# Seven tap weights spread by a matmul, and a tile that moves from 256-token steps to a 512-token step

## The chip, the core and the metric

The kernel runs on one core of one Trainium2 chip. The metric is the device time of one execution in microseconds (us): 690.42 for the kernel before, the median of three runs from 689.95 to 690.78. The profiled execution has a span of 688.2 us; all times inside the kernel are counted from the start of that span.

## What is computed

Tokens are rows of 192 numbers; there are 8 sequences of 4096 tokens. A causal convolution with 7 taps, whose weights are a softmax over the taps and differ for each of 8 groups of 24 channels, is followed by a feed-forward block of width 2048 with a Silu whose argument is scaled by a beta for each of its channels.

```python
w = exp(weight - max(weight, -1)); w = w / sum(w)            # weight: 8 groups x 7 taps
conv[b, s, h, :] = sum_k w[h, k] * x_pad[b, s + k, h, :]     # x: 8 x 4096 x 192, 6 zero rows in front
h = conv @ w_in                                              # 192 x 2048
out = (h / (1 + exp(-beta * h))) @ w_out                     # 2048 x 192
```

## The kernel before

Two streams of 16,384 tokens each are worked on side by side; a step of n tokens means n tokens of each stream. The steps are 128, 128 and 256 tokens for the first tile of 512, then 256 tokens up to the end of the fourth tile, then 512 tokens for the other 28 tiles. `pin` keeps an instruction in program order on its engine.

```python
steps = [(0, 128), (128, 128), (256, 256)]
NP = len(steps)
steps += [(t, 256) for t in range(TILE, 4 * TILE, 256)]      # steps 3 to 8
NQ = len(steps)                                              # 9
steps += [(t, TILE) for t in range(4 * TILE, TS, TILE)]      # steps 9 to 36
```

The head of the kernel builds the taps. Each tap weight is wanted on every partition that holds a channel of its group, so a load repeats every row of `weight` eight times for each stream. The Exp of the taps makes seven diagonal matrices; TensorE uses them for the convolution of the first tile, on x that it has transposed itself.

```python
for s, eng in enumerate((nc.sync, nc.scalar)):
    pin(eng.dma_start(out=x0[:, 0, s, :], in_=xs[s, 0:128, :]))
for s, eng in enumerate((nc.sync, nc.scalar)):
    pin(eng.dma_start(out=taps[half_of(s), :],
                      in_=weight[:, None, :].to_broadcast([H, Q // H, K])))
# ... beta16 and x0[1] follow on sync; w_in, xb0, w_out, xb1, xf on gpsimd
pin(nc.scalar.activation(scrap, one, AF.Exp))                # brings the Exp table in
# ... ident by memset and affine_select
warm(9, 256)                                                 # matmuls on ones
pin(nc.vector.tensor_reduce(out=nmax, in_=taps, axis=AX.X, op=ALU.max, negate=True))
pin(nc.scalar.activation(etap, taps, AF.Exp, bias=nmax, accum_out=tsum))
for k in range(2): make_diag(k)                              # diag[k] = ident2 * etap[:, k]
t = transpose_0(pa[0], x0, 0)                                # 3 TensorE transposes
take_0(t, 0, act=True)                                       # xr <- PSUM, on ScalarE
warm(6, 128)
for k in range(2, K): make_diag(k)
pin(nc.scalar.activation(scrap, one, AF.Silu))               # brings the Silu table in
conv_0(b0, 0)                                                # 7 taps x 2 streams of matmuls
evac_0(b0, 0, 0, nc.scalar); evac_0(b0, 0, 1, nc.vector)     # xcp <- PSUM
t1 = transpose_0(pa[1], x0, 1)
# ... transpose of beta, then first_tile() weaves the other blocks into steps 0 and 1
```

From the second tile on, VectorE does the convolution (`tap`, 7 instructions for a 256-token step, 21 for a 512-token step), up to two steps ahead of TensorE and ScalarE. In a step, `mm1` makes 16 chunks of h, ScalarE applies the Silu to each, and the second product runs one step behind. It has two forms. After a 256-token step it is `mm2`, with tokens as rows of the output, taken out by a VectorE copy. From the step NQ on, the output is transposed (`mm2_quarters`) and taken out by a VectorE stream transpose; this form needs `w_out_q`, a rearranged copy of w_out that VectorE makes once.

```python
for i in range(n_steps):
    plan = mm2_plan(i - 1) if NP <= i <= NQ else [[] for _ in range(NF)]
    for u in range(NF):
        mm1(i, u)                              # 6 or 12 matmuls, then one Silu
        for t in plan[u]: mm2(i - 1, *t)
        if i > NQ: mm2_quarters(NM)
        vector_work(i, 1307 * steps[i][1] // TILE, flush=u == NF - 1)
# the queue of VectorE work: for each step its fetch, at NQ + 1 the w_out_q copies, its conv
    if i == NQ + 1:
        work += [(i, 330, lambda c=c, m=m: part_w_out(c, m)) for c in range(0, NF, 4) for m in range(NM)]
    work += conv_ops(i)
```

Of the kernel before, what the change touches and what calls it, by code (L numbers as in the profile page):

```python
# [10 lines left out]
FP32 = mybir.dt.float32  # L11
FP32R = mybir.dt.float32r
BF16 = mybir.dt.bfloat16
AF = mybir.ActivationFunctionType
ALU = mybir.AluOpType
AX = mybir.AxisListType
# [3 lines left out]
def kernel(  # L20
# [9 lines left out]
    nc = tc.nc  # L30

    B, S, D = x.shape
    H, K = weight.shape
# [5 lines left out]
    Q = D // NK  # L39
    NS = 2  # L40
    TS = B * S // NS
    TILE = 512
# [3 lines left out]
    def pin(ins):  # L46

        return tc.keep_in_program_order(ins)
# [4 lines left out]
    consts = ctx.enter_context(tc.tile_pool(name="consts", bufs=1))  # L53
# [11 lines left out]

    steps = [(0, 128), (128, 128), (256, 256)]
    NP = len(steps)
    steps += [(t, 256) for t in range(TILE, 4 * TILE, 256)]
    NQ = len(steps)
    steps += [(t, TILE) for t in range(4 * TILE, TS, TILE)]  # L70
    n_steps = len(steps)


# [35 lines left out]
    def half_of(s):  # L109
        return slice(64 * s, 64 * s + 64)  # L110
# [8 lines left out]
    x0 = consts.tile([128, 2, NS, D], FP32, name="x0")  # L119
    xb0 = consts.tile([128, 2, NS, D], BF16, name="xb0")  # L120
    xb1 = consts.tile([128, 2, NS, D], BF16, name="xb1")
    taps = consts.tile([128, K], FP32, name="taps")
    for s, eng in enumerate((nc.sync, nc.scalar)):
        pin(eng.dma_start(out=x0[:, 0, s, :], in_=xs[s, 0:128, :]))  # L124
    for s, eng in enumerate((nc.sync, nc.scalar)):
        pin(eng.dma_start(out=taps[half_of(s), :],
                          in_=weight[:, None, :].to_broadcast([H, Q // H, K])))
    beta16 = consts.tile([NF, 128], FP32, name="beta16")
    pin(nc.sync.dma_start(out=beta16, in_=moe_beta.rearrange("(c p) -> c p", p=128)))
    HF = F // 2  # L130
# [1 line left out]
    def load_x0(b, eng):  # L132
# [7 lines left out]
    scrap = consts.tile([128, 1], FP32, name="scrap")  # L140
    pin(nc.scalar.activation(scrap, one, AF.Exp))

    ident = consts.tile([128, 128], FP32, name="ident")
    pin(nc.vector.memset(ident, 0.0))
    pin(nc.gpsimd.affine_select(out=ident, in_=ident, compare_op=ALU.not_equal, fill=1.0,
                                base=0, pattern=[[-1, 128]], channel_multiplier=1))
    for f0, f1 in ((0, 256), (256, 640), (640, HF)):
# [7 lines left out]
    for s in range(NS):  # L155
        pin(nc.gpsimd.dma_start(out=xb1[:, :, s, :],
                                in_=xs[s, TILE:TILE + 256, :].rearrange("(b p) d -> p b d", p=128)))
# [21 lines left out]
    def warm(n, cols):  # L179
        for _ in range(n):  # L180
            pin(nc.tensor.matmul(idle[:, 0, 0:cols], ones[:, 0:128], ones[:, 0:cols], start=True, stop=True))

    warm(9, 256)
    cv0 = psum_h.tile([128, 2, TILE], FP32, name="ph")
    nmax = consts.tile([128, 1], FP32, name="nmax")
    pin(nc.vector.tensor_reduce(out=nmax, in_=taps, axis=AX.X, op=ALU.max, negate=True))
    etap = consts.tile([128, K], FP32, name="etap")
    tsum = consts.tile([128, 1], FP32, name="tsum")
    pin(nc.scalar.activation(etap, taps, AF.Exp, bias=nmax, accum_out=tsum))  # L189
    diag = consts.tile([128, K, NS, Q], FP32R, name="diag")  # L190

    def make_diag(k):
# [10 lines left out]
    def transpose_0(bank, src, b):  # L203

        bf = src.dtype == BF16
        t = (bank.bitcast(BF16) if bf else bank)[:, 0:NK * 128].rearrange("p (k t) -> p k t", k=NK)
        v = src[:, b, :, :].rearrange("p s d -> p (s d)").rearrange("p (m k) -> p k m", k=NK)
        for kk in range(NK):
            pin(nc.tensor.transpose(t[:, kk, :], v[:, kk, :], ident_b if bf else ident))  # L209
        return t  # L210

    def take_0(t, b, act=False):
        dst = xr[:, :, PAD + 128 * b:PAD + 128 * b + 128]
        if act:
            pin(nc.scalar.activation(dst, t, AF.Copy))  # L215
        else:
            pin(nc.vector.tensor_copy(dst, t))
# [20 lines left out]
    pb = po_banks()  # L238
    t = transpose_0(pa[0], x0, 0)
    take_0(t, 0, act=True)  # L240
    warm(6, 128)
    for k in range(2, K):
        make_diag(k)
    rsum = consts.tile([128, 1], FP32, name="rsum")
# [219 lines left out]
    for i in range(NP, n_steps):  # L464
        j = steps[i][0] // TILE + 1
# [140 lines left out]
```

## Time and profile before

| what | value |
|---|---|
| device time, median of 3 | 690.42 us |
| span of the profiled execution | 688.2 us |
| TensorE matmul (PE) busy | 681.2 us, 99% |
| weight loads (PEld), beside the matmuls | 451.1 us, 66% |
| ScalarE (ACT) busy | 586.5 us, 85% |
| VectorE (DVE) busy | 553.2 us, 80% |
| GpSimd (POOL) busy | 14.1 us, 2% |
| granted TensorE clock, all 40 slices | 0.9 or more |
| first Silu of step 0 / 3 / 9 / 10 / 11 starts at | 11.54 / 34.14 / 97.97 / 114.40 / 135.12 us |

Busy time is an average over stages that differ. The first Silu of a step, read in the timeline of ScalarE, cuts the span into steps; the length of a step is the distance to the next one. In the timeline a line has its start, its length, the engine, the line of the program and the tiles (out<-in), a count where several alike were merged, and in brackets the idle time of the engine before it, with what ended it. SPq, ACTq and POOL lines with DMA are the issue of a transfer, not the transfer.

### The profile page before, as it was taken

How to read it: one execution, taken by the hardware profiler on the slowest of the kernel's cores; microseconds unless marked ns; L12 is line 12 of the kernel's file. 1: busy time of each engine (PE TensorE's matmuls, PEld its weight loads, DVE VectorE, ACT ScalarE, POOL GpSimd, SP SyncE). 2: the span in 40 equal slices, each digit the busy share in tenths (PEclk: the TensorE clock that was granted, in tenths of full speed). 3: DMA queues.
4: the chain of work that ended last, by engine and by line, in shares of the span. 5: the costliest groups of instructions: out<-in, count | busy, mean ns of one | idle time of the engine just before them, and what ended most of it. 6: DMA issues, size and time to landing. Idle time of an engine off the chain costs nothing.

```text
span 688.2 us, 27039 instructions
## 1 busy us (share of the span) xinstructions
PE 681.2 (99%) x12426; PEld 451.1 (66%) x12426; DVE 553.2 (80%) x902; ACT 586.5 (85%) x600; POOL 14.1 (2%) x25
## 2 busy tenths in 40 slices
PE   7999999999999999999999999999999999999998
PEld 5799986555555555555555555555555567777777
DVE  4999999999998889878889888888888898875112
ACT  5999999888888888888888888888888888888881
POOL 7000000000000000000000000000000000000000
PEclk9999999999999999999999999999999999999999
DMA  9554333354334344323344323444224443220113
GB/s 212 157 139 113 89 105 90 89 134 108 102 76 106 105 118 117 80 62 106 105 117 116 79 63 106 105 117 116 72 70 105 106 117 71 56 55 12 48 49 92
DMA packets 148977, 66.84 MB, mean 97 GB/s; under 512 B 110672, under 2 KB 148256, under 8 KB 148864
## 3 DMA queue, kind: packets, MB, share of 16 engines
q1 hardware_dynamic: 145480, 61.08, 34.5%
q0 software_dynamic: 3168, 3.93, 2.7%
q8 instruction: 97, 1.59, 1.0%
q14 instruction: 16, 0.13, 0.1%
q10 hardware_dynamic: 216, 0.10, 0.0%
HBM read 28.32 MB, written 25.17 MB: 78 GB/s over the span
## 4 chain that ended last, share of the span: by engine, by line
PE 97%; ACT 1%; DMA 1%; DVE 0%; issue 0%; SPq 0%; DVEq 0%
PE ph L330 47%; PE po L408 41%; PE po L362 6%; PE po L446 2%; PE ph L313 1%; ACT gp L317 1%; DMA taps<-in_weight_dram 1%; ACT g L317 1%; PE ph L223 0%; PE po L209 0%; PE po L223 0%; ACT etap L189 0%; SPq L124 0%; ACT xr L215 0%; DVE o_sp L368 0%
## 5 line engine op out<-in xcount | busy, mean ns | idle before, releaser
L334 ACT ACTIVATE g<-ph,beta 128x1024 bf16<-128x1024 f32 (+1 forms) x544 | 560.4, 1038 | 79.0 <-PE ph L330 63.4
L330 PE MATMUL ph<-xc,w_in_s 64*64 64x512 bf16 (+2 forms) x5856 | 589.3, 366 | 0.3 <-ACT g L317 0.3
L408 PE MATMUL po<-g,w_out_q 64*64 64x512 bf16 x5184 | 528.5, 376 | 0.0
L330 PEld LDWEIGHTS <-w_in_s 64*64 64x64 bf16 (+1 forms) x5856 | 271.5, 104 | 126.8 <-issue 0.5
L296 DVE SCALAR_TENSOR_TENSOR acc<-xt,tapn,acc 128x512 f32<-128x512 bf16 (+1 forms) x450 | 311.3, 763 | 0.9
L408 PEld LDWEIGHTS <-w_out_q 64*64 64x64 bf16 x5184 | 240.0, 105 | 91.9
L425 DVE STREAM_TRANSPOSE o_sb<-po 128x512 f32<-128x512 f32 x81 | 72.0, 889 | 110.3 <-PE po L408 110.3
L296 DVE SCALAR_TENSOR_TENSOR xc<-xt,tapn,acc 128x512 bf16<-128x512 bf16 (+1 forms) x90 | 64.1, 763 | 0.1
L362 PE MATMUL po<-w_out_s,g 64*128 64x192 bf16 x896 | 57.1, 243 | 0.0
L86 DVE CAST xb<-xf 128x768 bf16<-128x768 f32 (+1 forms) x62 | 48.7, 824 | 0.0
L362 PEld LDWEIGHTS <-g 64*128 64x128 bf16 x896 | 43.4, 94 | 3.3
L294 DVE TENSOR_SCALAR acc<-xt,tapn 128x512 f32<-128x512 bf16 (+1 forms) x90 | 41.0, 488 | 1.1
L368 DVE COPY o_sp<-po 128x192 f32<-128x192 f32 x40 | 12.7, 350 | 9.7 <-PE po L446 7.3
L313 PE MATMUL ph<-xcp,w_in_s 64*128 64x256 bf16 (+1 forms) x144 | 15.0, 316 | 0.2 <-ACT gp L317 0.2
L317 ACT ACTIVATE gp<-ph,beta 128x256 bf16<-128x256 f32 x32 | 12.4, 479 | 1.8 <-PE ph L313 1.8
L446 PEld LDWEIGHTS <-g 128*128 128x128 bf16 x128 | 10.5, 98 | 0.4 <-issue 0.4
L446 PE MATMUL po<-w_out_s,g 128*128 128x192 bf16 x128 | 10.7, 246 | 0.0
L317 ACT ACTIVATE g<-ph,beta 128x512 bf16<-128x512 f32 x16 | 9.6, 692 | 0.2
L313 PEld LDWEIGHTS <-w_in_s 64*128 64x128 bf16 x144 | 6.8, 97 | 3.6 <-issue 1.0
L223 PE MATMUL po<-xr,diag 64*128 64x384 f32 x49 | 8.9, 401 | 0.0
L362 PE MATMUL po<-w_out_s,gp 64*128 64x192 bf16 x128 | 7.2, 243 | 0.0
L362 PEld LDWEIGHTS <-gp 64*128 64x128 bf16 x128 | 5.8, 94 | 1.6
(49 smaller groups left out, 60.1 us busy)
## 6 DMA issues: line engine op xcount, KB each, us to landing
xf<-in_x_dram SPq DMA_DIRECT2D x60, 384.0 KB, 3.9
out_dram<-o_sb SPq DMA_DIRECT2D x108, 192.0 KB, 4.6
out_dram<-o_sp SPq DMA_DIRECT2D x16, 192.0 KB, 4.1
xt<-xb SPq DMA_TRANSPOSE x122, 3.0
w_out_f<-in_moe_w_out_dram POOLq DMA_DIRECT2D x4, 384.0 KB, 7.3
w_in_s<-w_in_s POOLq DMA_DIRECT2D x4, 192.0 KB, 6.0
out_dram<-o_sp SPq DMA_DIRECT2D x8, 96.0 KB, 1.6
w_in_s<-in_moe_w_in_dram POOLq DMA_DIRECT2D x4, 144.0 KB, 4.9
```

The source lines that it names most:

```text
L86: pin((eng or nc.vector).tensor_copy(xbf_of[j][:, b0:b1, :, s, :].rearrange("p b k q -> p k b q"), xf_of[j][:, b0:b1, s, :].rearrange("p b ...
L294: pin(nc.vector.tensor_scalar_mul(a, src, w))
L296: pin(nc.vector.scalar_tensor_tensor(out=xc_of[i][:, k0:k1, 0:n] if k == K - 1 else a, in0=src, scalar=w, in1=a, op0=ALU.mult, op1=ALU.add))
L313: pin(nc.tensor.matmul(ph[:, h, 0:NS * n], w_in_s[half_of(h), kk, ts(fcs[h], 128)], xc_of[i][half_of(h), :, kk, :], start=(kk == 0), stop= ...
L317: pin(nc.scalar.activation(g_at(i, fcs[h])[:, :, 0:n], ph[:, h, 0:NS * n].rearrange("p (s t) -> p s t", s=NS), AF.Silu, scale=beta[:, fcs[ ...
L330: pin(nc.tensor.matmul(ph[m0:m1, s, 0:n], w_in_s[half_of(s), kk, 128 * fc + m0:128 * fc + m1], xc_of[i][half_of(s), kk, 0:n], start=(kk == ...
L334: pin(nc.scalar.activation(g_at(i, fc)[:, :, 0:n], ph[:, :, 0:n], AF.Silu, scale=beta[:, fc:fc + 1]))
L362: pin(nc.tensor.matmul(po[q][:, 0:D], g_at(i, fc)[r, s, ts(b, 128)], w_out_s[r, fc, :], start=(phase == 0 and fc == 0), stop=(phase == 1 a ...
L368: pin(nc.vector.tensor_copy(dst, po[:, 0:D]))
L408: pin(nc.tensor.matmul(po_of[i, m][half_of(s), 0:n], w_out_q[half_of(r), fc, m, :], g_at(i, fc)[half_of(r), s, 0:n], start=(first and fc = ...
L425: pin(nc.vector.transpose(osb_of[i][:, 0:n // L, :, m], po_of[i, m][:, 0:n].rearrange("p (b l) -> p b l", l=L)))
L446: pin(nc.tensor.matmul(po[:, 0:D], g_at(i, fc)[:, s, ts(b, 128)], w_out_s[:, fc, :], start=(fc == 0), stop=(fc == NF - 1)))
```

## The change

Two independent things are done.

The first is in the head. The taps are loaded as they are, 8 rows of 7 numbers, by one transfer that goes first on its queue. A matrix `sel` of zeros and ones (8 x 128) is built by a memset and a second affine_select, and one matmul `sel` x taps spreads the eight rows over 128 partitions into PSUM, from where the maximum and the Exp read them. Three small warming matmuls follow it, and seven instead of six follow the transposes. The transfer of taps that ScalarE's queue issued is gone, and x0's first half is now the second transfer on sync. It is for starting the convolution of the first block earlier.

The second moves `NQ` from 9 to 7: the fourth tile is one step of 512 tokens in place of two of 256, so that the kernel has 36 steps, 29 of them of 512 tokens. All that hangs on NQ moves along: the first 512-token step (with `mm2` of the step before it) is step 7, `w_out_q` is made in the queue of step 8, and `mm2_quarters` begins in step 8.

```diff
-    steps += [(t, 256) for t in range(TILE, 4 * TILE, 256)]
+    steps += [(t, 256) for t in range(TILE, 3 * TILE, 256)]
     NQ = len(steps)
-    steps += [(t, TILE) for t in range(4 * TILE, TS, TILE)]
+    steps += [(t, TILE) for t in range(3 * TILE, TS, TILE)]
...
-    taps = consts.tile([128, K], FP32, name="taps")
+    taps = consts.tile([H, K], FP32, name="taps")
+    pin(nc.sync.dma_start(out=taps, in_=weight))
     for s, eng in enumerate((nc.sync, nc.scalar)):
         pin(eng.dma_start(out=x0[:, 0, s, :], in_=xs[s, 0:128, :]))
-    for s, eng in enumerate((nc.sync, nc.scalar)):
-        pin(eng.dma_start(out=taps[half_of(s), :],
-                          in_=weight[:, None, :].to_broadcast([H, Q // H, K])))
...
+    sel = consts.tile([H, NS, H, Q // H], FP32, name="sel")
+    pin(nc.vector.memset(sel, 0.0))
     ident = consts.tile([128, 128], FP32, name="ident")
     pin(nc.vector.memset(ident, 0.0))
+    pin(nc.gpsimd.affine_select(out=sel, in_=sel, compare_op=ALU.not_equal, fill=1.0, base=0,
+                                pattern=[[0, NS], [-1, H], [0, Q // H]], channel_multiplier=1))
...
-    pin(nc.vector.tensor_reduce(out=nmax, in_=taps, axis=AX.X, op=ALU.max, negate=True))
+    tap_ps = cv0[:, 1, 0:K]
+    pin(nc.tensor.matmul(tap_ps, sel.rearrange("h s g j -> h (s g j)"), taps, start=True, stop=True))
+    warm(3, 128)
+    pin(nc.vector.tensor_reduce(out=nmax, in_=tap_ps, axis=AX.X, op=ALU.max, negate=True))
-    pin(nc.scalar.activation(etap, taps, AF.Exp, bias=nmax, accum_out=tsum))
+    pin(nc.scalar.activation(etap, tap_ps, AF.Exp, bias=nmax, accum_out=tsum))
...
-    warm(6, 128)
+    warm(7, 128)
```

## The prediction

> **What bounds the kernel now.** I read the chain that ended last first, to see where the span is set; then the timeline of the head; then the steps one by one. The chain in order of time (start, length, what):
>
> ```profile
> 1.19 4.75 DMA taps<-in_weight_dram
> 7.09 0.66 PE ph L223
> 9.70 0.84 PE po L209 x3
> 10.75 1.25 PE ph L313 x12
> 14.92 2.30 ACT gp L317 x6
> ```
>
> The kernel's first 6 us hang on the transfer of seven tap weights. Then come the first convolution (L223), two groups of matmuls, and from 11.54 on the Silus of step 0. From 11.54 to 97.6 ScalarE is busy without gaps worth naming, so there a shift of the first Silu shifts everything. From the first step with quarters on, TensorE sets the pace: 20.72 us a step to the end. So the head counts in full, unless a later load catches it. The timeline of the head:
>
> ```profile
> 0.74 0.39 SPq L124 DMA_DIRECT2D x<-in_x_dram  x1
> ...
> 1.19 0.80 SPq L126 DMA_DIRECT2D taps<-in_weight_dram  x1
> 1.19 1.20 ACTq L126 DMA_DIRECT2D taps<-in_weight_dram  x1
> ...
> 3.44 0.88 PE L209 MATMUL po<-ident,x 128*128 128x128 f32 x3 [0.58 <-DMA x<-in_x_dram]
> ...
> 6.04 0.16 DVE L186 TENSOR_REDUCE nmax<-taps 128x1 f32<-128x7 f32 x1 [4.18 <-DMA taps<-in_weight_dram]
> 6.23 0.30 ACT L189 ACTIVATE etap<-taps,nmax 128x7 f32<-128x7 f32 x1 [2.31 <-DVE nmax L186]
> ...
> 6.53 0.47 ACT L215 ACTIVATE xr<-po 128x384 fp32r<-128x384 f32 x1
> ...
> 7.09 0.66 PE L223 MATMUL ph<-xr,diag 64*128 64x384 f32 x1 [2.14 <-ACT xr L215]
> ```
>
> What to see: the transposes of x were done at 4.32, but their copy to `xr` stands behind `etap` in ScalarE's order, and `etap` behind the taps. TensorE idles 2.14 us on it. The steps, as busy time of each engine in windows cut at the first Silu of steps 7, 8, 9 and 10 (window, length, then busy us and count of PE, PEld, DVE, ACT, POOL):
>
> ```profile
> 76.50:87.10 10.60, 10.60 (x230) 10.57 (x226) 10.10 (x20) 10.52 (x17) 0.00 (x0) 1.00 0.36 88
> 87.10:97.90 10.80, 10.80 (x228) 10.46 (x224) 9.76 (x21) 10.49 (x16) 0.00 (x0) 1.00 0.38 117
> 97.90:114.40 16.50, 16.50 (x235) 10.73 (x232) 16.46 (x34) 16.36 (x16) 0.00 (x0) 1.00 0.34 92
> 114.40:135.10 20.70, 20.70 (x380) 12.43 (x380) 20.63 (x37) 17.82 (x16) 0.00 (x0) 1.00 0.32 81
> ```
>
> The 256-token steps and the first 512-token step are ScalarE's (10.52 of 10.60, 16.36 of 16.50); the quarter steps are TensorE's, ScalarE having 17.82 of 20.70. VectorE is full in both of the last two windows. That matters for the second half of the change.
>
> **What the Trainium skill says.** "DMA: Bandwidth & Descriptors", section "Anatomy of one DMA": a transfer costs about 2.0 us however small, mostly waiting for the write's receipt. The trace has that form: the two halves of x, issued at 0.74, landed at 3.19 and 3.35, that is 2.45 and 2.61 us; the repeated taps, many pieces of 28 bytes, needed 4.75. "ScalarE: Activation LUTs", "What ACT_TABLE_LOAD costs": about 1283 ns; the trace has 1.28 us, twice, in the head. "TensorE: Matmul & The Clock Gate", Part 1: the array runs at half rate until one window of 3.4 us was busy, the windows run freely, and (Part 4) transposes don't count as busy. The trace agrees with a late switch: 256-column matmuls start 213 ns apart up to 11.6 us and 107 ns apart after, and TensorE idled from 2.9 to 3.4 and from 5.0 to 7.1. Nothing in the trace shows that transposes don't count.
>
> **Part 1, the head.** Taps now go out at 0.74. With the 2.45 us of the x half they land near 3.1 (their issue shouldn't exceed that half's 0.39). The x half behind them goes out 0.4 later and lands near 3.6. `sel` needs a memset and a select ahead of `ident`'s (the present select takes 0.29), ready near 1.4, no wait. The spreading matmul I put at 0.25 (the 16-column transpose of beta took 0.28): over at 3.35. `nmax` 0.16 and `etap` 0.30, with the gaps of today (0.06, 0.03): `etap` is over at 3.9. ScalarE is free for it, since its table load no longer stands behind a taps issue of 1.20: today it ran 2.42 to 3.70, now from 1.2 to 2.5. First diagonal at 4.3 (0.13 wait and 0.244 each, 1.71 for seven).
>
> The transposes start at 3.65 and end at 4.5, and now they, not the taps, end the wait of `xr`: 4.55 to 5.05. The seven warming matmuls (0.107 apart) end near 5.3. **The first convolution starts at 5.25 in place of 7.09: 1.85 us earlier.** The added matmul, memset and select lie beside the wait for x.
>
> From there two things decide what arrives. First the clock. If the windows lie as in this trace, they end at 11.6, 8.2 and 4.8. With no long gap after 4.8, the array is at full rate by 8.2 at the latest. The convolution at half rate takes 2.6 us as now (7.09 to 9.70) and ends at 7.85; evacuation 0.65 (Silu table then long loaded); then the first mm1 and Silu, today 0.86 apart, 0.5 at full rate. First Silu at 9.1 in place of 11.54: 2.4 earlier. Were the clock full already by 4.8, the diagonals (0.244 each) would pace the convolution and the first Silu could come near 8.4.
>
> Second, the loads. Landings I worked out from the trace and moved 0.3 later for the second select: first w_in pieces 6.2 and 6.7 (wanted 8.6), x block 1 near 7.0 (wanted 7.85), x blocks 2 and 3 9.2 and 9.7 (wanted from 9.5 and 10.5), last w_in piece 12.4 (wanted by u=5, at 15.07 today, so at 12.6), w_out 13.3 to 17.1 (wanted 13.9 on). A gain of 2.4 just passes; over 2.7 the last w_in piece stops it. **I take 2.2 us**, between the bare 1.85 and 2.4.
>
> **Part 2, the steps.** Two 256-token steps go: first Silus at 65.94 and 87.08, so 21.14 for the pair. One quarter step is added: 20.72 (114.40 to 135.12). **Gain 0.42 us.** The ScalarE-bound first 512-token step of 16.4 is there before and after, only two steps earlier.
>
> Does VectorE keep up? Before, it made `xc` of step 9 by 93.19, 3.7 us ahead, and of step 10 only by the moment it was wanted:
>
> ```profile
> 97.81 1.70 DVE L269 COPY w_out_q<-w_out_s 128x256 bf16<-128x256 bf16 x8
> ...
> 111.28 2.06 DVE L296 SCALAR_TENSOR_TENSOR xc<-xt,tapn,acc 128x512 bf16<-128x512 bf16 x3
> 113.27 1.60 DVE L86 CAST xb<-xf 128x768 bf16<-128x768 f32 x2
> ```
>
> Step 10's mm1 began at 113.52. After the change, in times without the head's shift: VectorE ends conv of step 6 at 57.95 and, with the 16.1 us that casts and conv of step 9 took (76.67 to 93.19 without 0.44 of waiting), has step 7's at 74.0, wanted at 75.6. Then copies of w_out 2.6, casts 1.6, out-copies 1.6 and conv 13.3: step 8's at 93.1. It is wanted at about 92.9 (step 7's first Silu at 76.9 plus 16.0). So VectorE, one tile earlier in its run, is still just in time, or 0.2 late. A stall there is paid in full, as TensorE sets the pace from then on. **I charge 0.2 us.**
>
> **Sum:** 690.42 - 2.2 - 0.42 + 0.2 = 687.99, say 688.0.
>
> **Rivals.**
> 1. The x transfer takes the place of the taps: pushed behind them, it lands later than 3.6, or the seven warming matmuls delay the convolution. For it: the diff puts the taps first on that queue. Each 0.1 us late costs 0.1. If x lands at 4.5, the head gains 1, and the time is 689.2.
> 2. Loads catch the head: w_in and the x blocks arrive 0.3 later, and the gain stops at 1.5 or so. For it: DMA engines are at nine tenths from 3 us on. Against: today nothing after 6 us waits for one on TensorE. The time: 688.7.
> 3. VectorE misses step 8 by more, 1 us or more, because its lead is shorter: every 256-token tile gave it some lead (10.1 of 10.6 busy), and one such tile is gone. The time: 689 to 689.5.
> 4. The clock opens at 4.8: another 0.3 to 0.5, 687.5.
>
> **Range and chances.** The terms I am unsure of are the head (1.5 to 2.8) and the stall (0 to 1). Together they give 687.2 to 689.5; the three runs of before differ by 0.8, so I take 687.0 to 689.6. 2% is 13.8 us, five times the whole effect: within 2% 0.98, faster 0.01, slower 0.01.
>
> **What would show it.** `nmax` no longer waits for a DMA but for TensorE, before 3.7; `xr` is released by the transposes; first convolution at 5.2 to 5.4; 256-column matmuls 107 ns apart from about 8.2; first Silu near 9.2 to 9.5; step 7 of 16.4 and then 20.72 each; little or no wait of TensorE for `xc` at step 8. A DMA wait of TensorE between 9 and 13, or a wait for `xc`, would prove rivals 2 or 3. I'd be wrong altogether if the step period of 20.72 changed, which nothing here touches.

## The result and the profile after

The changed kernel took 686.97 us (median of 4 runs, 686.85 to 687.65) beside 690.6 for the kernel before (4 runs, 689.95 to 690.98): a ratio of 0.995, 95% interval 0.9933 to 0.9968. Repeated with more runs it took 687.25 (22 runs) beside 688.86 (67 runs): 0.9976, interval 0.9966 to 0.9985. So the change is worth about 1.6 us, well within 2%. The time after is the same both times; what moved is the kernel before, whose single runs lie anywhere from 687.0 to 692.7. Part of the reason is shown below; it matters for every number here.

The chain that ended last, in the changed kernel (start, length, what):

```profile
1.75 2.56 POOL w_in_s L113 x4
4.32 4.88 DMA xb<-in_x_dram
12.22 2.30 ACT gp L323 x6
```

The taps are gone from the chain. In their place stands another transfer, the one of x block 2 (`xb`), and ahead of it four issues of w_in on GpSimd's queue. The timeline of the changed head:

```profile
0.74 0.41 SPq L123 DMA_DIRECT2D taps<-in_weight_dram  x1
...
2.79 0.59 PE L190 MATMUL ph<-taps,sel 8*128 8x7 f32 x2
...
3.42 0.17 DVE L192 TENSOR_REDUCE nmax<-ph 128x1 f32<-128x7 f32 x1 [1.20 <-PE ph L190]
...
4.49 0.49 ACT L221 ACTIVATE xr<-po 128x384 fp32r<-128x384 f32 x1 [0.52 <-PE po L215]
...
5.13 0.44 PE L229 MATMUL ph<-xr,diag 64*128 64x384 f32 x1
...
7.47 0.83 PE L319 MATMUL ph<-xcp,w_in_s 64*128 64x256 bf16 x12
...
8.01 1.57 ACT L323 ACTIVATE gp<-ph,beta 128x256 bf16<-128x256 f32 x4 [0.76 <-DVE xr L223]
...
9.24 0.35 PE L215 MATMUL po<-ident_b,xb 128*128 128x128 bf16 x3 [0.94 <-DMA xb<-in_x_dram]
```

What to see: `nmax` waits for TensorE, `xr` for the transposes. The convolution starts at 5.13, and twelve mm1 matmuls take 0.83 in place of 1.32: the array is at full rate. The first Silu comes at 8.01, 3.53 earlier than before. Then, at 9.24, TensorE stands 0.94 us for x block 2. The steps, in windows cut at the first Silus of steps 6, 7, 8 and 9 (length, then PE, PEld, DVE, ACT, POOL busy):

```profile
63.30:74.20 10.90, 10.90 (x231) 10.56 (x226) 10.90 (x23) 10.52 (x17) 0.00 (x0) 1.00 0.42 129
74.20:90.60 16.40, 16.40 (x233) 10.62 (x231) 16.36 (x36) 16.31 (x16) 0.00 (x0) 1.00 0.36 98
90.60:111.40 20.80, 20.80 (x380) 14.79 (x380) 20.73 (x37) 17.88 (x17) 0.00 (x0) 1.00 0.34 82
```

The sequence of steps is the old one, one tile earlier. VectorE has `xc` of step 8 ready just in time; the next cast shows when it was free:

```profile
88.00 2.07 DVE L302 SCALAR_TENSOR_TENSOR xc<-xt,tapn,acc 128x512 bf16<-128x512 bf16 x3
89.99 1.61 DVE L86 CAST xb<-xf 128x768 bf16<-128x768 f32 x2
```

The marks by which all profiles below are compared (us from the span's start):

| kernel | nmax starts | convolution of block 0 | first Silu of step 0 | of step 1 | span |
|---|---|---|---|---|---|
| before, first profile | 6.04 | 7.09 to 9.70 | 11.54 | 17.95 | 688.2 |
| before, second profile | 4.87 | 5.92 to 8.53 | 10.17 | 16.51 | 686.8 |
| changed, first profile | 3.42 | 5.13 to 6.64 | 8.01 | 15.25 | 685.2 |
| changed, second profile | 3.41 | 5.11 to 6.62 | 8.00 | 15.23 | 685.3 |
| before, with warming matmuls | 4.93 | 5.99 to 7.59 | 8.96 | 15.30 | 685.6 |
| changed, without warming | 3.42 | 4.81 to 7.42 | 9.27 | 15.96 | 685.9 |
| third tile at 512 too | 3.41 | 5.13 to 7.59 | 8.96 | 15.30 | 693.5 |
| matrix copied from identity | 3.42 | 5.08 to 6.59 | 7.96 | 14.94 | 684.9 |
| and x block 2 first | 3.41 | 5.11 to 6.63 | 8.00 | 15.09 | 685.1 |

### The profile page after: what moved, and what is told of

Read it like the earlier page. It is cut to its first block, busy times and chain, and to the rows that moved or that the text cites. A ratio compares the mean times of both kernels' runs of the same rounds, so it can differ in the third digit from the quotient of the medians.

```text
span 685.2 us, 26902 instructions
## 1 busy us (share of the span) xinstructions
PE 679.8 (99%) x12368; PEld 501.6 (73%) x12368; DVE 553.0 (81%) x905; ACT 584.0 (85%) x584; POOL 14.6 (2%) x26
## 4 chain that ended last, share of the span: by engine, by line
PE 97%; ACT 1%; DMA 1%; POOL 0%; issue 0%; DVE 0%; POOLq 0%
PE ph L336 47%; PE po L414 42%; PE po L368 4%; PE po L452 2%; PE ph L319 1%; ACT gp L323 1%; DMA xb<-in_x_dram 1%; ACT g L323 1%; POOL w_in_s L113 0%; PE po L229 0%; PE po L215 0%; POOL sel L146 0%; DVE o_sp L374 0%; POOL ident L148 0%; POOLq L146 0%
## 5 line engine op out<-in xcount | busy, mean ns | idle before, releaser
L336 PE MATMUL ph<-xc,w_in_s 64*64 64x512 bf16 (+2 forms) x5856 | 573.2, 369 | 0.3 <-ACT g L323 0.3
L336 PEld LDWEIGHTS <-w_in_s 64*64 64x64 bf16 (+1 forms) x5856 | 303.8, 105 | 95.2 <-issue 0.6
L414 PEld LDWEIGHTS <-w_out_q 64*64 64x64 bf16 x5376 | 289.4, 106 | 72.3
L431 DVE STREAM_TRANSPOSE o_sb<-po 128x512 f32<-128x512 f32 x84 | 74.7, 889 | 113.0 <-PE po L414 112.9
L368 PE MATMUL po<-w_out_s,g 64*128 64x192 bf16 x640 | 40.8, 243 | 0.0
L368 PEld LDWEIGHTS <-g 64*128 64x128 bf16 x640 | 31.0, 94 | 3.3
L374 DVE COPY o_sp<-po 128x192 f32<-128x192 f32 x32 | 10.2, 350 | 7.3 <-PE po L452 7.3
```

What stands on the lines that cost most here:

```text
L336: pin(nc.tensor.matmul(ph[m0:m1, s, 0:n], w_in_s[half_of(s), kk, 128 * fc + m0:128 * fc + m1], xc_of[i][half_of(s), kk, 0:n], start=(kk == ...
L368: pin(nc.tensor.matmul(po[q][:, 0:D], g_at(i, fc)[r, s, ts(b, 128)], w_out_s[r, fc, :], start=(phase == 0 and fc == 0), stop=(phase == 1 a ...
L374: pin(nc.vector.tensor_copy(dst, po[:, 0:D]))
L414: pin(nc.tensor.matmul(po_of[i, m][half_of(s), 0:n], w_out_q[half_of(r), fc, m, :], g_at(i, fc)[half_of(r), s, 0:n], start=(first and fc = ...
L431: pin(nc.vector.transpose(osb_of[i][:, 0:n // L, :, m], po_of[i, m][:, 0:n].rearrange("p (b l) -> p b l", l=L)))
```

## The experiments

**Each half alone.** The edit of the first keeps the old steps in the changed kernel, that of the second makes only the new steps in the kernel before:

```diff
 # head alone (in the changed kernel)      # steps alone (in the kernel before)
-range(TILE, 3 * TILE, 256)               -range(TILE, 4 * TILE, 256)
+range(TILE, 4 * TILE, 256)               +range(TILE, 3 * TILE, 256)
```

> The head of the change alone, with the fourth tile still in two 256-token steps. If the two halves of the change simply add, and the head brought 2.68 us by the first Silu of step 3 (34.14 before, 31.46 after): first Silus of steps 0 to 3 as in the changed kernel (8.0, 15.25, 21.9, 31.5), span 688.2 - 2.7 = 685.5, and 2.7 us faster than before. Rival, that the head is paid back later because a stage further on waits for a load or for VectorE: the first Silus of steps 3 to 9 drift back toward those of before, and less than 2 us is left at the end.

> The step half alone, on the old head. First theory (two steps of 10.57 out, one of 20.72 in, and a wait for xc of at most 0.1): 0.35 us faster than before, step 7 of 16.5 us, then 20.72 each. Rival (VectorE's shorter lead costs as much as the step saves, or more): no gain or a loss of up to 0.5, with a wait of TensorE or its weight loads for xc at step 8 of 0.5 or more.

Measured: the head alone 687.47 (21 runs) beside 688.72 (65 runs), ratio 0.9984, interval 0.9977 to 0.9991: 1.1 us, not 2.7. Its profile is as expected, first Silus 7.86, 15.29, 21.95 and 31.48, span 685.6, and nothing drifts back. So the rival isn't the reason: the base was another. The steps alone took 689.29 (13 runs), ratio 1.0008, interval 0.9998 to 1.0018. By the time this is a miss: 0.35 us faster would be 0.9995, outside the interval. The profile shows the gain all the same. From the first Silu of step 3 (33.79) to that of step 8 (92.98) it took 59.19; the kernel before needs for the same tokens 34.14 to 93.68 (114.40 less one step of 20.72), 59.54. That is the expected 0.35. It stands in the other profiles too: from the first Silu of step 1 to the end, the five with the old steps take 670.26 to 670.33, the eight with the new ones (the run with a third tile aside) 669.93 to 670.07. So the step half is worth about 0.3, and whatever else sets these profiles apart lies ahead of step 1. What the head did in the other twelve runs of the steps alone is not known.

**What the first comparison was worth.** The changed kernel, the head alone and the kernel before were run once more, beside each other, unchanged.

> The changed kernel once more, beside runs of the kernel before on the same chip. The first comparison had four runs of each and gave 3.6 us (ratio 0.995); beside the later runs, in which the kernel before took 688.7 and 689.0, the head alone gave 1.2 us. Theory of the varying head (the kernel before differs from run to run by when the taps land, 4.9 to 6.0 in three profiles, and by when the array's rate doubles, while the changed kernel waits for x block 2 near 9.2 whatever happened earlier): changed kernel 686.9 to 687.2 with a spread under 1 us, kernel before near 688.7 with a spread of 4, ratio 0.9972 to 0.9982. Rival (the first four runs were typical): 3 us or more, ratio under 0.9960.

> The head alone once more, to stand beside the changed kernel on the same chip; the two differ in the fourth tile's steps only. Trace theory (21.14 us of two steps give way to 20.72, and the first 512-token step is 0.07 longer): the changed kernel is faster than this by 0.35 us. Rival (the step half is worth nothing, as the run of it alone, 1.0008, could be read): the two are equal within 0.1.

> The kernel before, unchanged, for a second profile of it. Theory of the varying head: ratio 1.000 within 0.001, and the profile's first Silu and taps do not repeat the first profile's 11.54 and 5.98; where the time is 688.5 or below, the taps came earlier or the 256-column matmuls were already 107 ns apart at their first. Rival (the head repeats, and the chips differ): first Silu within 0.2 of 11.54.

Measured: 687.25 (22 runs, all but one within 686.7 to 687.7), ratio 0.9976; head alone 687.64 (14 runs), ratio 0.9986, interval 0.9974 to 0.9997; before against itself 688.94 and 688.86, ratio 1.0006, interval 0.9996 to 1.0016. Changed kernel and head alone lie 0.39 apart in their medians, as the trace's 0.35 says; the intervals alone would not part them. The theory of the varying head holds for the two profiles of the kernel before. In the second:

```profile
4.87 0.16 DVE L186 TENSOR_REDUCE nmax<-taps 128x1 f32<-128x7 f32 x1 [3.01 <-DMA taps<-in_weight_dram]
...
5.92 0.65 PE L223 MATMUL ph<-xr,diag 64*128 64x384 f32 x1 [1.17 <-ACT xr L215]
...
9.51 0.94 PE L313 MATMUL ph<-xcp,w_in_s 64*128 64x256 bf16 x12
```

The taps came 1.17 earlier than in the first profile, and the rate changed in the middle of the twelve mm1 matmuls (0.94, between 1.32 and 0.83). That execution took 688.56, the first 690.01; the first Silu of step 1 came 1.44 earlier, which is the whole difference. In the eight profiles with the new load in which the matrix is not made late, `nmax` starts at 3.41 or 3.42. The change removes a spread as well as a time. Two things stay open: no execution near 687.0 or 692.7 was profiled, and only 10 of these 67 runs are as slow as the fastest of the first four, so why all four were is not known.

**Is it the clock?** The array's rate is read here from the distance between the starts of matmuls. The granted clock of the windows does not show it: in the first profile of before it reads 1.00 from 3 to 8 us, where the pairs of convolution matmuls start 0.32 apart, against 0.18 in the changed kernel. Warming matmuls alone were added to the kernel before, and taken out of the changed one:

```diff
 # in the kernel before                    # in the changed kernel
-warm(9, 256)                             -warm(3, 128)
+warm(9, 256); warm(4, 128)               -warm(7, 128)
-warm(6, 128)
+warm(28, 128)
```

> The kernel before, with the old repeated load of the taps, and only warming matmuls added: four of 128 columns while x is awaited, and 28 in place of 6 while the taps are awaited. The convolution cannot start before 7.1. Clock theory (a good part of the head's gain came because TensorE had no long idle stretch, so its array went to full rate at about 5 in place of 11.6): convolution of block 0 in 1.5 to 1.7 us in place of 2.6, first Silu near 9.7 to 10.1 in place of 11.54, and 1.4 to 1.8 us faster than before. Start theory (the gain is the earlier start alone, the rate changes on its own schedule): first Silu at 11.5 or a little later, time as before within 0.3.

> The changed kernel without the three and the seven warming matmuls. They are left out, nothing else. Clock theory: TensorE then idles from about 4.5 to 5.1 and the array may stay at half rate; the convolution starts at 5.1 all the same but takes 2.6 us, first Silu at 9.2 to 9.6 in place of 8.0; since the loads hold step 0 back to 9.24 anyway, only 0.3 to 0.8 us of time is lost. Rival (half a microsecond of idleness is too short to matter): convolution in 1.3 to 1.5 us, first Silu at 8.0, time as the changed kernel's, 687.0.

The timeline of TensorE in the kernel before with warming:

```profile
3.87 1.81 PE L181 MATMUL ph<-const-bfloat16-1.0 128*128 128x128 bf16 x28
5.99 0.41 PE L224 MATMUL ph<-xr,diag 64*128 64x384 f32 x1 [0.31 <-ACT xr L216]
...
8.42 0.83 PE L314 MATMUL ph<-xcp,w_in_s 64*128 64x256 bf16 x12
9.19 0.35 PE L210 MATMUL po<-ident_b,xb 128*128 128x128 bf16 x3
```

687.8 (21 runs, 687.25 to 688.14), ratio 0.9983, interval 0.9975 to 0.9990: 0.9 us faster and a spread of 0.9 in place of 4.3, by idle work alone. The repeated load of the taps is still there, so its landing alone does not make a spread of 4.3. The convolution took 1.60 in place of 2.61. The taps had come early in this profile (4.93), so the second profile of before is the one to compare with: same taps, 1.21 earlier at the first Silu of step 0 and at that of step 1. The clock theory is right in kind; I expected 1.4 to 1.8. The transposes of x block 2 (the last line) wait for no load here: the block had landed at 8.38. The changed kernel without its warming:

```profile
4.81 0.68 PE L228 MATMUL ph<-xr,diag 64*128 64x384 f32 x1 [0.58 <-ACT xr L220]
...
8.40 1.46 PE L317 MATMUL ph<-xcp,w_in_s 64*128 64x256 bf16 x12
```

Half rate again (1.46 for the twelve), 1.26 later at the first Silu and 0.71 at that of step 1: 687.49 (21 runs), ratio 0.9981, interval 0.9973 to 0.9989. By the medians of two chips that is 0.2 from the changed kernel, less than the 0.7 of the profiles, and the intervals overlap. On its own chip the head alone took 687.47, as much, though it lacks the step half; with 0.3 for that half the warming is worth about 0.3, an estimate. In this profile the array stayed slow after an idle stretch of 0.58 us; but the profile with the third tile at 512 has no such stretch and was slow until 7.2, so the stretch is not the only cause. That leaving the warming out costs 0.3 to 0.8 us of time is not shown.

**Is it the loads that take it back?** Four edits around GpSimd's queue:

```diff
 # 1: first w_in pair ahead of the identity's select, matrix copied from the identity (later)
 # 2: as 1, and x block 2 ahead of the second w_in pair
 # 3: identity's select first, matrix copied from it, order of the loads untouched
-pin(nc.vector.memset(sel, 0.0))
-pin(nc.gpsimd.affine_select(out=sel, ...))
+for s in range(NS):
+    pin(nc.vector.tensor_copy(sel[:, s, :, :], ident[0:H, 0:H, None].to_broadcast([H, H, Q // H])))
 # 4: as 3, and x block 2 ahead of the second w_in pair
```

> The changed kernel, with GpSimd's queue freed: the first pair of w_in loads is issued ahead of the select that makes the identity, and the spreading matrix is copied from the identity by two small VectorE copies in place of a memset and a second select. All later loads are issued about 0.65 earlier. Load theory (3.5 us were won at the first Silu but 0.85 was lost again because TensorE waited until 9.24 for x blocks 2 and 3): these transposes start near 8.6, first Silu stays at 8.0 to 8.2, first Silu of step 1 near 14.7 in place of 15.25, and 0.5 us faster than the changed kernel. Rival (the transfers are bound by bandwidth from 4 us on, so an earlier issue moves their landing little): the transposes stay at 9.0 or later and the time moves by less than 0.2.

> As the run with loads issued early, and x block 2 goes ahead of the second pair of w_in loads, block 3 behind it. If landing follows the order of issue: block 2 lands near 7.6, the w_in pair near 8.7, so TensorE waits for neither by more than 0.3, first Silu of step 1 near 14.3, and 0.9 to 1.1 us faster than the changed kernel. Rival (the bytes that step 0 needs are the limit, in whatever order): the wait moves from the x block to w_in, and the time stays within 0.2 of the run with loads issued early.

Both missed. The first took 687.57 (9 runs), the second 688.13 (21 runs). My edit was at fault. GpSimd issues its first load at 1.26, not 0.75; after two issues of 0.7 and the select the next went out at 2.96, 0.12 earlier than in the changed kernel. The matrix came late, `nmax` at 4.03, TensorE idle 0.54 ahead of the spreading matmul, and the convolution, from 5.75, at half rate in all but its end or throughout. Nothing about the loads follows from these two.

> The changed kernel, with the spreading matrix copied from the identity by two small VectorE copies; its memset and its select are gone, so the loads on GpSimd's queue are issued at 1.42 in place of 1.72, and the matrix is still there before the taps. Load theory (the landing of x block 2 holds step 0): the block lands near 8.9 in place of 9.2, its transposes start near 8.95, first Silu of step 1 near 14.95 in place of 15.25, 0.3 us faster than the changed kernel. Rival (bandwidth: the landing stays where it is however early the issue): transposes at 9.2 and the time of the changed kernel.

Measured: 687.0 (22 runs, 686.6 to 687.7), ratio 0.9977, interval 0.9967 to 0.9986; beside the changed kernel's 687.25 in the same comparison the intervals don't part them, the profile does. The transposes of x block 2:

```profile
8.93 0.35 PE L214 MATMUL po<-ident_b,xb 128*128 128x128 bf16 x3 [0.67 <-DMA xb<-in_x_dram]
```

The block landed at 8.88, its transposes began at 8.93, step 1 at 14.94: the expected numbers to 0.02. Issued 0.3 earlier, landed 0.3 earlier, everything after it 0.3 earlier. In this profile and in the first of the changed kernel the wait shows that the landing of x block 2 sets step 0; in the second of the changed kernel block 3 did as well (landed 10.15, transposed from 10.19). That the earlier issue moves the landing rests on one profile: in six with the issue at 4.32 or 4.31 the block landed from 9.05 to 9.40, so 8.88 is below them all; but with the old load of the taps and the issue at 4.02 or 4.01 it landed from 8.34 to 9.11 in four.

> The run with the spreading matrix copied from the identity (687.0), and in addition x block 2 goes ahead of the second pair of w_in loads, block 3 behind it. If landing follows the order of issue and x block 2 was what held step 0: block 2 lands near 8.1 in place of 8.9, the w_in pair near 9.2 in place of 8.3, so the second chunk's mm1 starts at 9.2 in place of 9.49, first Silu of step 1 near 14.65, and 0.2 to 0.3 us faster. Rival (all the bytes of step 0 are the limit, in whatever order): the wait moves from the x block to w_in or to block 3, and the time stays within 0.1 of 687.0 or gets longer.

Measured: 687.03 (13 runs), ratio 0.9971, interval 0.9959 to 0.9982; step 1 at 15.09, not 14.65. The transposes of blocks 2 and 3:

```profile
8.23 0.35 PE L215 MATMUL po<-ident_b,xb 128*128 128x128 bf16 x3
...
9.83 0.35 PE L215 MATMUL po<-ident_b,xb 128*128 128x128 bf16 x3 [0.18 <-DMA xb<-in_x_dram]
```

Block 2 landed at 7.62 and nobody waits for it now, but w_in's pair landed at 8.40 and 9.10 and block 3 at 9.78. The rival is right in this run: the wait moved to the loads that were put behind, and this order gains nothing.

**How near is VectorE to its limit?** One more tile goes to a 512-token step:

```diff
-range(TILE, 3 * TILE, 256) / range(3 * TILE, TS, TILE)
+range(TILE, 2 * TILE, 256) / range(2 * TILE, TS, TILE)
```

> The changed kernel with the third tile too as one 512-token step. VectorE theory (its lead over TensorE is what the 256-token tiles build up, and the change has used nearly all of it): xc of step 5 comes near 54.1 where it is wanted at 51.8, xc of step 6 near 73.4 where it is wanted at 71.2, so two waits of about 2.2 us each against 0.42 saved; about 4 us slower than the changed kernel, between 3 and 5. Rival (each tile moved to 512 saves its 0.42, VectorE keeps up): 686.6, with no wait for xc.

Measured: 694.8 (4 runs), ratio 1.0079, interval 1.0064 to 1.0094, 7.6 slower than the changed kernel's 687.25 on another chip. Direction right, size not. The waits, in total, times and longest:

```profile
PE ph L336 <- DVE xc L302: 4.7, 5, 2.5
```

then the timeline of VectorE, and a window of all engines in which TensorE's granted clock is the 0.57:

```profile
68.61 0.62 DVE L374 COPY o_sp<-po 128x192 f32<-128x192 f32 x2 [2.98 <-PE po L368]
```

```profile
75.00:79.00 4.00, 3.61 (x30) 1.64 (x32) 3.96 (x9) 1.11 (x1) 0.57 0.15 49
```

I had counted two late `xc`. But VectorE, once late, then waited 2.98 itself: in its order an out-copy of step 4 stands ahead of the rest of the convolution, and that output was late because step 5 was. And after its stop of 2.49 TensorE had, for the next 4 us, little over half its clock. So here a late `xc` cost itself, a mutual wait and a slow array.

## Why the prediction was right, and where it was not

The time 686.97 lies 0.03 below the lower end of the range 687.0 to 689.6 and 1.0 below the point; the repeat, 687.25, lies inside. The parts of the mechanism were right (an earlier start, then a limit by a load, then a small gain by the steps); the sizes met the sum partly by luck.

- **The start.** 5.25 predicted, 5.13 measured. Two errors cancel on the way: the spreading matmul started at 2.79 without a wait for the taps, which I had landing at 3.1, and it appears twice and takes 0.59, not 0.25. So `nmax` came at 3.42, against 3.41 (3.35 and a gap of 0.06).
- **The clock.** This is the mis-sized term. I let the windows lie as in the first trace and took the convolution at half rate, 2.6 us; it took 1.51. That was rival 4, to which I gave 0.3 to 0.5. In fourteen profiles the rate changed anywhere from under 3.9 to 11.7, so the first trace could not say when. Together with the faster mm1 the first Silu came at 8.01, not 9.1.
- **The loads.** My limit held in size: a gain of 2.4 passes, one over 2.7 is stopped. Of 3.53 at the first Silu 2.70 were left at step 1 (17.95 to 15.25). Where no load is waited for, step 1 follows step 0 by 6.34 in five profiles, and by 6.40 to 6.70 in three whose array was slow nearly to the end of the first chunk or longer; here it took 7.24, so the load cost 0.90. But it was x block 2, whose landing I had put at 9.2 (it was 9.20), and not w_in's last piece (11.48, no wait). By my own numbers the block, used at 11.94 before, stops a gain of 2.74; I had not worked that out. So rival 2 was real in kind, not in size: it let the gain stop at 1.5. The run with the third tile at 512 has the same head and a half-rate array until past 7: its first Silu is 0.95 later, that of step 1 only 0.05. So the wait for the load hides up to about 0.9 us of a slow array; without warming, where it was slow until 10.1, 0.71 came through.
- **The steps.** 21.14 for 20.72 held, and the period did not change. The stall was 0.07 (first 512-token step 16.50 in place of 16.43), not 0.2: net 0.35 against 0.22. In the second profile of the changed kernel that step took 16.62, a stall of 0.19.
- **The sum.** In the two first profiles 2.68 (first Silu of step 3, 34.14 to 31.46) and 0.35 make the 3.0 between the spans, 688.2 and 685.2; predicted 2.4. The head's 2.2 came near its 2.68 because two errors pull against each other: the first Silu came 1.1 earlier than I had worked out, and the wait of 0.9 that followed was not charged. That is luck. Against the second profile of before, 686.8, only 1.5 are left.
- **The base.** No term of mine stood for it: the 690.42 from which I subtracted lies high in the spread of the kernel before, whose median over 67 runs is 688.86. So the time came out close, the gain against the first runs was larger than predicted (3.6), and the gain against the typical run smaller (1.6). That too is luck: the same 2.4 taken from 688.86 would have missed by 0.8 on the other side (686.5).

Not settled: why the repeated load of taps ends the wait anywhere from 4.9 to 6.0 us. Neither its issue alone nor its contention with w_in was tried. Nor does any run tell why the rate changed by 5.1 in six of the seven profiles of the changed head that kept TensorE filled, and past 7 in one.

## What to carry to other kernels

Before a chain's first wait is removed, list the landing of each later load beside the moment at which the faster chain will want it: here the changed head brought the first Silu forward by 3.5 us against the first profile, and x block 2 let 2.7 of it through. Warming matmuls alone (0.9 us of time, against 1.1 for the changed head) also bring step 1 to 15.3, but without a wait for a load, so the two meet there for different reasons. The small load that repeated its rows was better loaded once and spread on chip: its user started at 2.79 without a wait in all eight profiles, where the repeated one was awaited until 4.9 to 6.0. When a change is worth less than the spread of the kernel before, read it from two profiles of each, mark by mark, and not from two medians.

## What the runs showed of the hardware that I had not expected

- Idle stretches of half a microsecond or more in the first 7 us went with a late full rate of TensorE's array. The seven profiles of the changed head without such a gap had it at the first convolution (5.0 to 5.1 us) in six cases and by 7.2 in one, the warmed old head by 3.9 (128-column matmuls 0.06 apart from there on); the six profiles with a gap between 7.6 and 11.7. This is how fourteen profiles fall, not a rule: 7.2 and 7.6 are close. The Trainium skill, "TensorE: Matmul & The Clock Gate", Part 1, gives a window of 3.4 us and half a microsecond of chance either way; here the switch moved over more than 7 us.
- A stop of 2.5 us in the middle of the kernel cost a second time: 512-column matmuls took 0.63 in place of 0.38 until 78.6, that is for 3.5 us after it had ended.
- A 32-bit matmul of 8 x 128 by 7 columns shows as two of 0.36 to 0.38 us, and together 0.59.
